# Eight gathers in a row, the gate's tiles in other PSUM banks, merge steps moved ahead of transposes

## The chip, the cores and the metric

The kernel runs on one core of one Trainium2 chip. The metric is the device time of one execution in microseconds; below it is given as the median of several executions. The core has five engines that each take their instructions in order: TensorE (PE in the profile, its weight loads PEld), VectorE (DVE), ScalarE (ACT), GpSimd (POOL) and SyncE (SP). DMAs are issued by SP, ACT or POOL, and each of these has a queue of its own.

## The reference

Attention with RMS-normalised queries and keys over 8 batches, 12 heads, 448 positions and 64 features, then a mixture of experts with a capacity: each of the 3584 tokens goes to its best expert of eight, and each expert keeps the 80 tokens with the largest gate weight. Tokens that are not kept give zero rows.

```python
def _attn_ref(q, k, v, g_q, g_k):
    q_n, k_n = rmsnorm(q, g_q), rmsnorm(k, g_k)
    scores = scale * np.matmul(q_n, k_n.transpose(0, 1, 3, 2))
    attn = softmax(scores)
    return np.matmul(attn, v)                       # x: tokens x 768 after a transpose
...
    logits = x @ w_gate
    expert_idx = np.argmax(logits, axis=1)
    gate_w = softmax(logits)[np.arange(N), expert_idx]
    for e in range(E):
        tok_idx = np.where(expert_idx == e)[0]
        if len(tok_idx) > capacity:
            keep = np.argpartition(-gate_w[tok_idx], capacity)[:capacity]
            tok_idx = tok_idx[keep]
        h = np.maximum(x[tok_idx] @ w1[e], 0.0)
        out[tok_idx] = gate_w[tok_idx, None] * (h @ w2[e])
```

## The kernel before, in words

**Attention.** Twelve heads of a batch are three groups of four, so there are 24 groups (`g`), each of seven rows of scores. The work is laid out by hand in 84 slots of two rows each, some 4.9 us long, plus a few before and after. A slot first computes the scores of its two rows (`score`, L312, into the PSUM pool `sc`, two buffers), ACT takes their exponentials (L315), DVE sums them up (`presum`, L339 and L341), and PE multiplies the rows of the slot before by `v` into `po` (`av`, L327; one buffer). Group `g` starts at slot b0 = 7g // 2, so an even group starts with a slot and an odd one in the middle of one. After its last row, ACT copies `po` to `us` (L332).

Three lists hold what else a slot does: `begins` (loads, before the scores), `mid` (between `presum` and `av`) and `end` (after `av`). The order of these lists is the program order of every engine. What matters here:

- Queries and keys of a group are prepared some slots ahead: ACT squares (L243, `mid`), DVE sums and scales them to `ms` (L252, L254), POOL raises them to the power -0.5 (`rs`, L261, at the `end` of two slots for each group), POOL multiplies (`qn`, L276, `mid`), PE transposes (`tp`, L288, `end`) into the PSUM pool `tp` (two buffers), ACT copies to `qkT` (L300, L302). The first group's squares and so on are cut in halves and spread over ACT, DVE and POOL. The gains `g_q` and `g_k` are four small DMAs from ACT's queue (L81, L82) that come after the group's first loads, and `gains` (L85) multiplies them.
- `xout` (L576 to L594) brings a group's result to rows of tokens: for `u` = 0 and then 1, four transposes of `us` into `xp` (pool `tp`), one ACT copy to `xb` (L586), and after the second, three DMAs from SP to the scratch tensor `xr_dram`. It comes at the `end` of slots b0+4 and b0+5 for an even group, b0+5 and b0+6 for an odd one. The last 64 columns of `us` are covered by the fourth transposition, which overlaps the third by 64.
- After the last group of a batch come `zl` (the logits and the sums of the softmax, L350, in the pool `tp`), its copy `zsb` (`gate1`), the transposition `zt` (`gate1t`, L365, pool `tp`) and the gate's arithmetic on DVE.
- The best 80 tokens of each expert are kept in a running list; the merge of a batch has six steps (`row`, `experts`, `own`, `counts`, `place`, `turn`) at the `end` of six slots one after the other. Each takes a PSUM buffer of the pool `sc` (`mp`) and an ACT copy out of it, and on DVE `beat` (L480, L483), `tied`, `ahead` (L514), `cnt` (L518), `put` and `keep`. They were put into the lists last, so they stand behind the slot's `rstd`, `xout` and `transp`.

**The last batch and the experts.** The last batch's gate and ranking is written out after the slots, with two buffers of `sc` for four tiles (`psb`, `pse`, `psa`, `psc`). It gives `idxT` (L798), the rows of the tokens of each expert. Then `gather` (L820) takes 80 rows of `xr_dram` by an indirect DMA from POOL's queue into `xg`, set to zero before (L815). `xpose` scales them (`xn`, L830) and transposes them (`xgT`). Two products per expert (L859, L874), the scaling `yo` (L877, three buffers) and a scatter (L882, indirect DMA from POOL's queue) follow. The scatters all write `out_dram`, so each waits for the landing of the one before.

Five of the gathers stand ahead of the first expert; the others follow one by one, each before the scatter of the expert that it stands in.

**Weights.** The first three experts' are loaded during the attention and stay. Those of the other five are brought to `wb_dram` as bf16 by POOL's queue during the attention, and fetched from there by SP (`fetch_late`) when space comes free: experts 4 and 5 by count from one at the end of the slots, the sixth's first matrix at the gate of the last batch, its second after the first `xpose` (a small `memset` of the tile sets the order), and the last two experts' after the products of the first two.

Of the kernel before, what the change touches and what calls it, by code (L numbers as in the profile page):

```python
# [20 lines left out]
def kernel(  # L21
# [50 lines left out]
    nc.scalar.activation(warm[:, 0:1], warm[:, 1:2], AF.Sqrt)  # L72
    ident = cpool.tile([128, 128], F32, name="ident")
    make_identity(nc, ident[:, :])
    identb = cpool.tile([128, 128], BF16, name="identb")
    gk2 = cpool.tile([128, 2], F32, name="gk2")
    gqk = cpool.tile([128, 1], F32, name="gqk")

    def load_g():
        for half in range(2):  # L80
            nc.scalar.dma_start(out=gk2[half * D:(half + 1) * D, 0:1], in_=g_q[:, None])  # L81
            nc.scalar.dma_start(out=gk2[half * D:(half + 1) * D, 1:2], in_=g_k[:, None])  # L82

# [122 lines left out]
    with av_stack:  # L206
# [111 lines left out]
        def av(r):  # L318
            g, x = divmod(r, RD)
            vt, at = st[g]["v"], st[g]["at%d" % x]  # L320
            if x == 0:
                st[g]["po"] = pops.tile([128, 2, 512], F32, tag="po", name="po")
            po = st[g]["po"]
            for u in range(2):
                p = slice(u * 64, u * 64 + 64)
                for hh in range(2):
                    nc.tensor.matmul(po[hh * D:(hh + 1) * D, u, :S],  # L327
                                     vt[p, hh * NX + x, :], at[p, hh, :],
                                     start=(x == 0), stop=(x == RD - 1))
            if x == RD - 1:  # L330
                st[g]["us"] = upool.tile([128, 2, S], F32, tag="us", name="us")
                nc.scalar.copy(st[g]["us"][:], po[:, :, :S])  # L332

# [9 lines left out]
        def zl(b, groups):  # L343

            if groups[0] == 0:
                gst[b]["zl"] = tpps.tile([128, 512], F32, tag="tp", name="zl")
            t = gst[b]["zl"]

            def mm(c, w, x, first, last):
                nc.tensor.matmul(t[32 * c:32 * c + 32, :S], w, x, start=first, stop=last)  # L350
            for i in groups:
                s = st[NQ * b + i]
                c = (2, 3) if i < 2 else (0, 1)
                for hh in range(2):
                    mm(hh, zsel[:, i, :], s["sm"][:, hh, :], i == 0, False)
                for u in range(2):
                    mm(c[u], wgs[:, 2 * i + u, :], s["us"][:, u, :], i == 0, i > 0)
# [4 lines left out]
        def gate1t(b):  # L362
            zt = tpps.tile([128, 512], F32, tag="tp", name="zt")
            for j in range(NJ + 1):
                nc.tensor.transpose(zt[:, j * 128:(j + 1) * 128],  # L365
                                    zsb[:, j * 128:(j + 1) * 128], ident[:, :])
            gst[b]["zt"] = zt
            if b < B - 1:
                zs = tpool.tile([128, 512], F32, tag="R", name="zs")
                nc.scalar.copy(zs[:, :], zt[:, :])  # L370
                gst[b]["zt"] = zs
# [84 lines left out]
        def merge(b):  # L456
# [80 lines left out]
            def vput():  # L537
# [6 lines left out]
                m["put"] = tpool.tile([128, NT, CAP], BF16, tag="put", name="put")  # L544
# [29 lines left out]
        def xout(g, u):  # L574
# [4 lines left out]
            for j in range(NJ + 1):  # L579
                c = j * 128 if j < NJ else S - 128  # L580
                nc.tensor.transpose(xp[:, j * 128:(j + 1) * 128], us[:, u, c:c + 128],  # L581
                                    ident[:, :])
            if u == 0:
                st[g]["xb"] = prep.tile([128, NJ + 1, 256], F32, tag="xb", name="xb", bufs=1)
            xb = st[g]["xb"]
            nc.scalar.copy(xb[:, :, u * 128:(u + 1) * 128],  # L586
                           xp[:, :].rearrange("p (j d) -> p j d", d=128))
# [4 lines left out]
            for t in range(2):  # L592
                nc.sync.dma_start(out=rows[:, t:SM // 64:2], in_=xb[64 * t:64 * t + 64, :NJ])
            nc.sync.dma_start(out=rows[:, NX - 1], in_=xb[64:, NJ])  # L594
# [52 lines left out]
        for b in range(B):  # L647
# [17 lines left out]
            for t, fs in enumerate(merge(b)):  # L665
                for f in fs:
                    at_slot(end, b0 + 8 + t, f)
# [3 lines left out]
        at_slot(begins, -10, load_g)  # L671
# [54 lines left out]
    pse = scps.tile([128, 2, 1024], BF16, tag="sc", name="pse")  # L726
# [7 lines left out]
    fetch_late(NW0 + 2, (0, ))  # L734
# [50 lines left out]
    put = tpool.tile([128, NT, CAP], BF16, tag="put", name="put")  # L785
    nc.vector.tensor_tensor(put[:], iota[:, :].unsqueeze(1).to_broadcast([128, NT, CAP]),
                            rank[:].unsqueeze(2).to_broadcast([128, NT, CAP]), op=ALU.is_equal)
    psc = scps.tile([128, 2, 512], F32, tag="sc", name="psc")
# [16 lines left out]
    NX0 = 5  # L805

    def rows(e):
        if e in (3, 4):
            return mpool.tile([CAP, XW], F32, tag="xg", name="xg")[:, :]
        return upool.tile([128, 2, S], F32, tag="us", name="xg")[:CAP].rearrange(  # L810
            "p u s -> p (u s)")[:, :XW]

    for e in range(NX0):
        xgs[e] = rows(e)
        nc.gpsimd.memset(xgs[e], 0.0)  # L815

    def gather(e):
        if e >= NX0:
            xgs[e] = rows(e)
# [24 lines left out]

    for e in range(NX0):
        gather(e)
    xpose(0)

    nc.vector.memset(w_tiles[NW0 + 2][1][:, 0, 0:2], 0.0)
    fetch_late(NW0 + 2, (1, ))  # L850
    for e in range(E):
# [15 lines left out]
        if e + NX0 < E:  # L867
            gather(e + NX0)
        DN = DM // 2
        yo = mpool.tile([CAP, DM], F32, tag="yo", name="yo", bufs=3)  # L870
# [51 lines left out]
```

## Time and profile before

| what | us |
|---|---|
| median of 3 runs | 500.81 (500.19 to 501.06) |
| the profiled execution | 498.67 |
| its span in the profile | 496.9 |
| ACT: first square of the first group (L243) starts | 6.38 |
| first scores (L312) start | 14.70 |
| `idxT` (L798) ends | 438.16 |
| first product of an expert (L859) starts | 445.89 |
| last scatter is issued (L882) | 491.77 |

The profile is of one execution. Its times are in microseconds from the start of the span; a line of the timeline has the start, the duration, the engine, the line of the program, the operation, output <- input, the shape and, in brackets, how long the engine stood idle before and what released it. A line of the groups has the total busy time, the mean of one in ns, and the idle time before them. The granted TensorE clock was 0.978 of full speed over the span.

The mean busy share of PE, 91%, is not even. In the attention, 15 to 395 us, it is busy 360.1 of 380.0 us; in the stretch of the experts, 440 to 497, 40.7 of 57.0. POOL is busy with 243.0 us in the former and 15.9 in the latter.

### The profile page before, as it was taken

How to read it: one execution, taken by the hardware profiler on the slowest of the kernel's cores; microseconds unless marked ns; L12 is line 12 of the kernel's file. 1: busy time of each engine (PE TensorE's matmuls, PEld its weight loads, DVE VectorE, ACT ScalarE, POOL GpSimd, SP SyncE). 2: the span in 40 equal slices, each digit the busy share in tenths (PEclk: the TensorE clock that was granted, in tenths of full speed). 3: DMA queues.
4: the chain of work that ended last, by engine and by line, in shares of the span. 5: the costliest groups of instructions: out<-in, count | busy, mean ns of one | idle time of the engine just before them, and what ended most of it. 6: DMA issues, size and time to landing. Idle time of an engine off the chain costs nothing. (4 is left out here: it accounts for less than half of the span.)

```text
span 496.9 us, 11200 instructions
## 1 busy us (share of the span) xinstructions
PE 451.0 (91%) x4527; PEld 222.3 (45%) x4527; DVE 358.0 (72%) x567; ACT 315.7 (64%) x491; POOL 267.7 (54%) x199
## 2 busy tenths in 40 slices
PE   6889999999899999699899999998998999869890
PEld 5334444353434444344344444443443444558770
DVE  4688756997899758776699669966976767445530
ACT  4777867877677768565787678767776666302210
POOL 2497883676555938618538835774578210242221
PEclk9799999999999999899999999999999999989996
DMA  6369979596958994994597959788939947779922
GB/s 217 117 136 300 254 184 251 97 291 183 243 121 222 230 256 74 267 162 159 172 167 247 254 166 241 188 218 200 238 98 220 211 90 264 281 214 354 372 98 60
DMA packets 68435, 100.84 MB, mean 203 GB/s; under 512 B 8480, under 2 KB 60192, under 8 KB 67104
## 3 DMA queue, kind: packets, MB, share of 16 engines
q1 hardware_dynamic: 52160, 70.54, 45.0%
q0 software_dynamic: 15616, 29.13, 32.9%
q8 instruction: 35, 0.57, 0.4%
q10 hardware_dynamic: 608, 0.46, 0.3%
q14 instruction: 16, 0.13, 0.1%
HBM read 101.12 MB, written 39.90 MB: 284 GB/s over the span
## 5 line engine op out<-in xcount | busy, mean ns | idle before, releaser
L261 POOL TENSOR_TENSOR rs<-ms,nhalf 128x14 f32<-128x14 f32 x46 | 136.5, 2970 | 130.2 <-DVE ms L254 124.0
L341 DVE TENSOR_TENSOR sm<-sm,at 128x896 f32<-128x896 f32 x120 | 155.6, 1297 | 24.1 <-ACT at L315 17.8
L315 ACT ACTIVATE at<-ps 128x896 f32<-128x896 f32 x168 | 147.8, 921 | 23.6 <-PE ps L312 19.2
L312 PE MATMUL ps<-qkT 64*64 64x448 f32 x1344 | 152.9, 561 | 9.6 <-ACT row L474 4.6
L327 PE MATMUL po<-at,vt 64*64 64x448 f32 x1344 | 145.4, 542 | 3.2 <-ACT us L332 3.2
L276 POOL TENSOR_TENSOR qn<-qk,rs 128x896 f32<-128x896 f32 (+1 forms) x45 | 84.5, 1894 | 8.3 <-DVE rs L267 8.2
L327 PEld LDWEIGHTS po<-at,vt 64*64 64x64 f32 x1344 | 50.2, 134 | 76.9 <-issue 67.0
L252 DVE TENSOR_REDUCE ms<-sq 128x14 f32<-128x896 f32 (+1 forms) x50 | 52.2, 1045 | 44.6 <-ACT sq L243 41.6
L312 PEld LDWEIGHTS ps<-qkT 64*64 64x64 f32 x1344 | 42.1, 134 | 73.7 <-issue 36.6
L288 PE MATMUL tp<-ident,qn 128*128 128x128 f32 x336 | 52.7, 280 | 5.1 <-DVE qn L276 3.5
L288 PEld LDWEIGHTS tp<-ident,qn 128*128 128x128 f32 x336 | 37.6, 142 | 32.0 <-issue 15.4
L586 ACT COPY xb<-xp 128x512 f32<-128x512 f32 x48 | 28.2, 588 | 36.6 <-PE xp L581 27.2
L243 ACT ACTIVATE sq<-qk 128x896 f32<-128x896 f32 (+1 forms) x50 | 45.9, 922 | 3.6 <-DMA qk<-in_k_dram 3.6
L581 PEld LDWEIGHTS xp<-ident,us 128*128 128x128 f32 x192 | 20.1, 140 | 34.7 <-issue 27.0
L300 ACT ACTIVATE qkT<-tp,gqk 128x512 f32<-128x512 f32 (+1 forms) x48 | 30.8, 643 | 4.7 <-PE tp L288 4.2
L302 ACT COPY qkT<-tp 128x384 f32<-128x384 f32 (+1 forms) x47 | 25.3, 538 | 12.0 <-PE tp L288 11.9
L581 PE MATMUL xp<-ident,us 128*128 128x128 f32 x192 | 31.5, 287 | 1.1 <-ACT xb L586 1.1
L863 ACT ACTIVATE h_sb<-ph 128x320 bf16<-128x320 f32 x16 | 7.0, 437 | 31.1 <-PE ph L859 31.1
L480 DVE TENSOR_SCALAR beat<-row,rg 128x128 bf16<-128x128 f32 (+3 forms) x28 | 23.2, 830 | 4.2 <-ACT row L474 3.8
L882 POOL DMA_INDIRECT out_dram<-yo,idxT x8 | 7.7, 963 | 34.2 <-DVE yo L877 14.9
L339 DVE TENSOR_TENSOR sm<-at 128x896 f32<-128x896 f32 x24 | 26.0, 1084 | 0.1
L332 ACT COPY us<-po 128x896 f32<-128x896 f32 x24 | 21.6, 902 | 5.8 <-PE po L327 5.8
(159 smaller groups left out, 407.9 us busy)
## 6 DMA issues: line engine op xcount, KB each, us to landing
wb_scratch<-in_moe_w_dram POOLq DMA_DIRECT2D x10, 1536.0 KB, 13.2
w_sb<-wb_scratch SPq DMA_DIRECT2D x10, 1536.0 KB, 11.1
vt<-in_v_dram SPq DMA_DIRECT2D x24, 448.0 KB, 6.1
out_dram<-zeros SPq DMA_DIRECT2D x28, 384.0 KB, 8.5
qk<-in_q_dram SPq DMA_DIRECT2D x23, 448.0 KB, 7.2
qk<-in_k_dram SPq DMA_DIRECT2D x23, 448.0 KB, 7.9
w_sb<-in_moe_w_dram POOLq DMA_DIRECT2D x6, 1536.0 KB, 15.3
xr_scratch<-xb SPq DMA_DIRECT2D x48, 192.0 KB, 5.5
```

The source lines that it names most:

```text
L243: nc.scalar.activation(st[g]["sq%d" % a][:, lo:hi], st[g]["qk"][a][:, lo:hi], AF.Square)
L252: nc.vector.reduce_sum(out=ms[:, lo:hi], in_=st[g]["sq%d" % a][:, lo:hi], axis=AX.X)
L261: nc.gpsimd.tensor_tensor(rs[:, lo:hi], ms[:, lo:hi], nhalf[:, lo:hi], op=ALU.pow)
L276: eng.tensor_mul(qn[:].rearrange("p (x hh) d -> p hh x d", hh=2)[:, h0:h1], qk[:, lo:hi].rearrange("p (hh x) d -> p hh x d", x=NX), rs[:, ...
L288: nc.tensor.transpose(tp[:, x * 128:(x + 1) * 128], qn[:, 2 * (x0 + x):2 * (x0 + x) + 2].rearrange("p h d -> p (h d)"), ident[:, :])
L300: nc.scalar.activation(o, i, AF.Copy, scale=gqk[:, :])
L312: nc.tensor.matmul(ps[u * 64:u * 64 + 64, hh, :S], T1[d, u, x * 64:(x + 1) * 64], T0[d, u, :], start=True, stop=True)
L315: nc.scalar.activation(at[:], ps[:, :, :S], AF.Exp)
L327: nc.tensor.matmul(po[hh * D:(hh + 1) * D, u, :S], vt[p, hh * NX + x, :], at[p, hh, :], start=(x == 0), stop=(x == RD - 1))
L341: nc.vector.tensor_add(s["sm"][:], s["sm"][:], s["at%d" % x][:])
L581: nc.tensor.transpose(xp[:, j * 128:(j + 1) * 128], us[:, u, c:c + 128], ident[:, :])
L586: nc.scalar.copy(xb[:, :, u * 128:(u + 1) * 128], xp[:, :].rearrange("p (j d) -> p j d", d=128))
```

## The change

- The four loads of the gains go from ACT's queue to POOL's, at the head of the program.
- A new tile `ul` holds the last 64 columns of both halves of `us`, copied by POOL right after `us`. One transposition of it replaces the two overlapping ones, so `xout` has four for `u` = 0 and three for `u` = 1; the copy to `xb` for `u` = 1 is 384 columns wide, not 512. The last DMA to the scratch is cut into two, since the last columns of the two halves now lie on different partitions.
- `zl` and `zt` take buffers of `sc`, not of `tp`. In the last batch `pse` and `psc` take that of `po`. `put` shares the buffer of `ahead`.
- The merge steps are put at the front of their slots' `end` lists, in the same order among themselves.
- All eight gathers stand in a row ahead of the first expert, each with a buffer of its own; the tiles for the first four are cleared by POOL, those for the last four by DVE. Both matrices of the sixth expert are fetched after the first `xpose`. `yo` has two buffers (the pool's default), not three.

```diff
@@ -70,17 +70,14 @@
     warm = cpool.tile([1, 2], F32, name="warm")
     nc.vector.memset(warm[:, :], 0.0)
     nc.scalar.activation(warm[:, 0:1], warm[:, 1:2], AF.Sqrt)
+    gk2 = cpool.tile([128, 2], F32, name="gk2")
+    gqk = cpool.tile([128, 1], F32, name="gqk")
+    for half in range(2):
+        nc.gpsimd.dma_start(out=gk2[half * D:(half + 1) * D, 0:1], in_=g_q[:, None])
+        nc.gpsimd.dma_start(out=gk2[half * D:(half + 1) * D, 1:2], in_=g_k[:, None])
     ident = cpool.tile([128, 128], F32, name="ident")
     make_identity(nc, ident[:, :])
     identb = cpool.tile([128, 128], BF16, name="identb")
-    gk2 = cpool.tile([128, 2], F32, name="gk2")
-    gqk = cpool.tile([128, 1], F32, name="gqk")
-
-    def load_g():
-        for half in range(2):
-            nc.scalar.dma_start(out=gk2[half * D:(half + 1) * D, 0:1], in_=g_q[:, None])
-            nc.scalar.dma_start(out=gk2[half * D:(half + 1) * D, 1:2], in_=g_k[:, None])
-
     def gains():
         nc.vector.tensor_mul(gqk[:, :], gk2[:, 0:1], gk2[:, 1:2])
         nc.vector.tensor_scalar_mul(gqk[:, :], gqk[:, :], 1.0 / math.sqrt(D))
@@ -330,6 +327,8 @@
             if x == RD - 1:
                 st[g]["us"] = upool.tile([128, 2, S], F32, tag="us", name="us")
                 nc.scalar.copy(st[g]["us"][:], po[:, :, :S])
+                st[g]["ul"] = prep.tile([128, 2, 64], F32, tag="ul", name="ul", bufs=1)
+                nc.gpsimd.tensor_copy(st[g]["ul"][:], st[g]["us"][:, :, SM:])
 
         def presum(r):
             g, x = divmod(r, RD)
@@ -343,7 +342,7 @@
         def zl(b, groups):
 
             if groups[0] == 0:
-                gst[b]["zl"] = tpps.tile([128, 512], F32, tag="tp", name="zl")
+                gst[b]["zl"] = scps.tile([128, 2, 512], F32, tag="sc", name="zl")[:, 0]
             t = gst[b]["zl"]
 
             def mm(c, w, x, first, last):
@@ -360,7 +359,7 @@
             nc.scalar.copy(zsb[:, :S], gst[b]["zl"][:, :S])
 
         def gate1t(b):
-            zt = tpps.tile([128, 512], F32, tag="tp", name="zt")
+            zt = scps.tile([128, 2, 512], F32, tag="sc", name="zt")[:, 0]
             for j in range(NJ + 1):
                 nc.tensor.transpose(zt[:, j * 128:(j + 1) * 128],
                                     zsb[:, j * 128:(j + 1) * 128], ident[:, :])
@@ -541,7 +540,7 @@
                 nc.vector.reduce_sum(out=rank[:], in_=rnk[:], axis=AX.X)
                 nc.vector.scalar_tensor_tensor(rank[:], rank[:], float(CAP), m["cnt"][:],
                                                op0=ALU.add, op1=ALU.subtract)
-                m["put"] = tpool.tile([128, NT, CAP], BF16, tag="put", name="put")
+                m["put"] = tpool.tile([128, NT, CAP], BF16, tag="ahead", name="put")
                 nc.vector.tensor_tensor(
                     m["put"][:], iota[:, :].unsqueeze(1).to_broadcast([128, NT, CAP]),
                     rank[:].unsqueeze(2).to_broadcast([128, NT, CAP]), op=ALU.is_equal)
@@ -576,22 +575,26 @@
             b, i = divmod(g, NQ)
             xp = tpps.tile([128, 512], F32, tag="tp", name="xp")
             us = st[g]["us"]
-            for j in range(NJ + 1):
-                c = j * 128 if j < NJ else S - 128
-                nc.tensor.transpose(xp[:, j * 128:(j + 1) * 128], us[:, u, c:c + 128],
-                                    ident[:, :])
+            for j in range(NJ):
+                nc.tensor.transpose(xp[:, j * 128:(j + 1) * 128],
+                                    us[:, u, j * 128:(j + 1) * 128], ident[:, :])
             if u == 0:
+                nc.tensor.transpose(xp[:, SM:512],
+                                    st[g]["ul"][:].rearrange("p u q -> p (u q)"), ident[:, :])
                 st[g]["xb"] = prep.tile([128, NJ + 1, 256], F32, tag="xb", name="xb", bufs=1)
             xb = st[g]["xb"]
-            nc.scalar.copy(xb[:, :, u * 128:(u + 1) * 128],
-                           xp[:, :].rearrange("p (j d) -> p j d", d=128))
+            n = NJ + 1 - u
+            nc.scalar.copy(xb[:, :n, u * 128:(u + 1) * 128],
+                           xp[:, :n * 128].rearrange("p (j d) -> p j d", d=128))
             if u == 0:
                 return
             rows = xr_dram[b * S:(b + 1) * S, i * 256:(i + 1) * 256].rearrange(
                 "(p x) d -> p x d", x=NX)
             for t in range(2):
-                nc.sync.dma_start(out=rows[:, t:SM // 64:2], in_=xb[64 * t:64 * t + 64, :NJ])
-            nc.sync.dma_start(out=rows[:, NX - 1], in_=xb[64:, NJ])
+                p = slice(64 * t, 64 * t + 64)
+                nc.sync.dma_start(out=rows[:, t:SM // 64:2], in_=xb[p, :NJ])
+                nc.sync.dma_start(out=rows[:, NX - 1, t * 128:(t + 1) * 128],
+                                  in_=xb[p, NJ, :128])
 
         def weights_early():
             qk_stack.close()
@@ -663,12 +666,11 @@
             at_slot(mid, b0 + 8, gate2i, b)
             at_slot(mid, b0 + 8, gate2p, b)
             for t, fs in enumerate(merge(b)):
-                for f in fs:
-                    at_slot(end, b0 + 8 + t, f)
+                for f in reversed(fs):
+                    end.setdefault(b0 + 8 + t, []).insert(0, (f, ()))
         at_slot(begins, 0, load_wgs)
         at_slot(end, NS - 3, weights_early)
         at_slot(end, NS, weights_late)
-        at_slot(begins, -10, load_g)
         at_slot(mid, 0, constants)
         at_slot(mid, -8, lambda: nc.scalar.activation(warm[:, 0:1], warm[:, 1:2], AF.Exp))
         for i in range(N // 128):
@@ -723,7 +725,7 @@
     gate2(b)
     gate2x(b)
     psb = scps.tile([128, 2, 512], F32, tag="sc", name="psb")
-    pse = scps.tile([128, 2, 1024], BF16, tag="sc", name="pse")
+    pse = pops.tile([128, 2, 1024], BF16, tag="po", name="pse")
     gate2i(b)
     for j in range(NT):
         nc.tensor.transpose(pse[:3 * E, 0, j * 128:(j + 1) * 128],
@@ -731,7 +733,6 @@
     eqT = tpool.tile([3 * E, 512], BF16, tag="cand", name="eqT")
     nc.scalar.copy(eqT[:, :], pse[:3 * E, 0, :512])
     gate2b(b)
-    fetch_late(NW0 + 2, (0, ))
     psa = scps.tile([128, 2, 512], F32, tag="sc", name="psa")
     gw = m["gw"]
     row = tpool.tile([128, 512], F32, tag="R", name="row")
@@ -782,10 +783,10 @@
                          m["eq"][:].rearrange("p j e -> p (j e)"))
     rank = gpool.tile([128, NT], F32, tag="rank", name="rank")
     nc.vector.reduce_sum(out=rank[:], in_=place[:], axis=AX.X)
-    put = tpool.tile([128, NT, CAP], BF16, tag="put", name="put")
+    put = tpool.tile([128, NT, CAP], BF16, tag="ahead", name="put")
     nc.vector.tensor_tensor(put[:], iota[:, :].unsqueeze(1).to_broadcast([128, NT, CAP]),
                             rank[:].unsqueeze(2).to_broadcast([128, NT, CAP]), op=ALU.is_equal)
-    psc = scps.tile([128, 2, 512], F32, tag="sc", name="psc")
+    psc = pops.tile([128, 2, 512], F32, tag="po", name="psc")
     o = psc[:CAP, 0, :2 * E]
     nc.tensor.matmul(o, identb[:CAP, :CAP], left[:].rearrange("p c e -> p (c e)"),
                      start=True, stop=False)
@@ -802,21 +803,18 @@
     mps = ctx.enter_context(tc.tile_pool(name="moe_ps", bufs=2, space=PSUM))
 
     xgs, xts, gws = {}, {}, {}
-    NX0 = 5
-
-    def rows(e):
-        if e in (3, 4):
-            return mpool.tile([CAP, XW], F32, tag="xg", name="xg")[:, :]
-        return upool.tile([128, 2, S], F32, tag="us", name="xg")[:CAP].rearrange(
-            "p u s -> p (u s)")[:, :XW]
-
-    for e in range(NX0):
-        xgs[e] = rows(e)
-        nc.gpsimd.memset(xgs[e], 0.0)
+    for e in range(E):
+        if e < 3:
+            xgs[e] = upool.tile([128, 2, S], F32, tag="us", name="xg")[:CAP].rearrange(
+                "p u s -> p (u s)")[:, :XW]
+        elif e < E - 1:
+            xgs[e] = mpool.tile([CAP, XW], F32, tag="xg", name="xg", bufs=E - 4)[:, :]
+        else:
+            xgs[e] = prep.tile([128, NJ + 1, 256], F32, tag="xb", name="xg", bufs=1)[
+                :CAP].rearrange("p j d -> p (j d)")[:, :XW]
+        (nc.gpsimd if e < 4 else nc.vector).memset(xgs[e], 0.0)
 
     def gather(e):
-        if e >= NX0:
-            xgs[e] = rows(e)
         nc.gpsimd.indirect_dma_start(
             out=xgs[e], out_offset=None, in_=xr_dram[:, :],
             in_offset=bass.IndirectOffsetOnAxis(ap=idxT[:, e:e + 1], axis=0),
@@ -842,12 +840,12 @@
         nc.vector.tensor_copy(xgT[:], pxt[:])
         xts[e] = xgT
 
-    for e in range(NX0):
+    for e in range(E):
         gather(e)
     xpose(0)
 
-    nc.vector.memset(w_tiles[NW0 + 2][1][:, 0, 0:2], 0.0)
-    fetch_late(NW0 + 2, (1, ))
+    nc.vector.memset(w_tiles[NW0 + 2][0][:, 0, 0:2], 0.0)
+    fetch_late(NW0 + 2)
     for e in range(E):
         w1_sb, w2_sb = w_tiles[e]
         h_sb = mpool.tile([128, FC, CAP], BF16, tag="hsb", name="h_sb")
@@ -864,10 +862,8 @@
                                  ph[:], AF.Relu)
         if e + 1 < E:
             xpose(e + 1)
-        if e + NX0 < E:
-            gather(e + NX0)
         DN = DM // 2
-        yo = mpool.tile([CAP, DM], F32, tag="yo", name="yo", bufs=3)
+        yo = mpool.tile([CAP, DM], F32, tag="yo", name="yo")
         for dn in range(2):
             py = mps.tile([CAP, DN], F32, tag="py", name="py")
             for fc in range(FC):
```

## The prediction

> **What bounds the kernel now.** I read the page first (busy shares, groups by line), then PE's waits, then two stretches of the timeline, then POOL and the DMA issues from 395 us on.
>
> ```profile
> span 496.9 us, 11200 instructions
> ...
> PE 451.0 (91%) x4527; PEld 222.3 (45%) x4527; DVE 358.0 (72%) x567; ACT 315.7 (64%) x491; POOL 267.7 (54%) x199
> ...
> L261 POOL TENSOR_TENSOR rs<-ms,nhalf 128x14 f32<-128x14 f32 x46 | 136.5, 2970 | 130.2 <-DVE ms L254 124.0
> ```
>
> By the table of windows PE is busy 360.1 of the 380.0 us from 15 to 395, the attention. It takes its work in program order, so a microsecond that it waits in the attention is taken as a microsecond of the span. The third line matters as much: POOL's `rs` (the power -0.5) takes 2.97 us each, and whatever is queued behind one waits that long.
>
> ```profile
> PE ps L312 <- ACT row L474: 4.6, 6, 0.9
> ...
> PE zl L350 <- ACT xb L586: 2.9, 7, 1.4
> ```
>
> These waits (total, times, longest) are what two of the edits go for. The end is another matter: the chain of waits has only the last two scatters, and before them POOL's queue goes by weights:
>
> ```profile
> 440.46 1.08 POOL L820 DMA_INDIRECT xg<-xr_scratch,idxT  x1 [10.40 <-DMA w_sb<-wb_scratch]
> ...
> 471.10 0.96 POOL L882 DMA_INDIRECT out_dram<-yo,idxT  x1 [7.34 <-DVE yo L877]
> 476.34 0.93 POOL L882 DMA_INDIRECT out_dram<-yo,idxT  x1 [4.28 <-DVE yo L877]
> 480.10 0.91 POOL L882 DMA_INDIRECT out_dram<-yo,idxT  x1 [2.83 <-issue]
> ...
> 491.77 0.91 POOL L882 DMA_INDIRECT out_dram<-yo,idxT  x1 [2.83 <-issue]
> ```
>
> Each scatter waits until the one before has landed. By the DMA issues, scatters issued at 451.5 and 461.6 took 9.2 and 8.7 us to land, that at 480.1 3.0. In between lie the weight fetches on SP's queue: issued 445.88 to 455.18, the last landed 19.7 us after its issue, at 474.9. From then scatters follow every 3.7 to 4.2 us to the end.
>
> **Gains, part by part.**
> (1) Start. ACT issues four small DMAs (1.74, 2.29, 4.92, 5.86, the last for 0.47), and its first square runs at 6.38, though the q halves had landed at 4.7 and 4.9. On POOL's queue they leave ACT free: its table is loaded at 2.53, the square starts at about 4.8. The k halves (5.9, 6.0) come in time for the third square. Gain 1.6, bounds 0 and 1.9: nothing if the gains land late, for `gqk` (10.56) already waits 0.36 for them; POOL needs some 1.0 us per issue (L171, L175), four in all, so they are out by about 5.
> (2) 24 transposes fewer, at 0.11 each (four in 0.44 at 399.53): 2.6. ACT's shorter second copy isn't PE's and costs or gains nothing.
> (3) `zl` leaves the `tp` buffers, so it no longer waits for the `xb` copy: 2.9 by PE's row, 4.6 by that of its weight loads; I take 3.8 (bounds 0, if the score buffers make it wait as long, and 4.6). `zt` waited 1.0 for the same copy, but comes right behind the `zsb` copy and its ACT result is needed as before: 0.
> (4) Merge steps first: ACT's `row` copy no longer stands behind `xb` and `qkT`, and `ps` waits less. In the odd batches the copy can be 0.65 earlier (`xp` at 135.12, `gw` ready at 134.74), in the even ones 0.24 (84.83 against 86.09, where PE is held for `gw` itself): 3 x 0.65 + 3 x 0.24 = 2.7, bounds 0 and the row's 4.6. The 4.2 for `move` are held by DVE, not by order: 0.
> Gains together 10.7.
>
> **Losses in the attention.** The 24 copies of `us`' last 64 columns go to POOL, and PE's fourth transposition of `xp` now waits for one. Alone such a copy is cheap: the nearest rows are L131's cast, 128x80 in 0.25, and `qn`, 1.89 for seven times the elements, 0.27; I take 0.3 and 0.1 to signal. The question is what is ahead of it in POOL's order. For an even group the `us` copy is in slot b0+4, and the `rs` of the slot before is ahead:
>
> ```profile
> 62.48 0.91 ACT L332 COPY us<-po 128x896 f32<-128x896 f32 x1 [0.25 <-PE po L327]
> ...
> 62.77 3.36 POOL L261 TENSOR_TENSOR rs<-ms,nhalf 128x14 f32<-128x14 f32 x1 [0.63 <-DVE ms L254]
> ...
> 64.60 0.66 PE L581 MATMUL xp<-ident,us 128*128 128x128 f32 x4
> ```
>
> `rs` ends at 66.13, the copy at 66.53; PE wants it at 64.60 + 3 x 0.11 = 64.93. PE stands 1.6 with the next scores behind it, which ACT, then `po`, wait for. So in groups 2, 8, 14 and 20: 6.4. Group 0 (`rs` 34.53 to 37.92, `xp` 36.58): 38.32 - 36.91 = 1.4. Groups 4, 10 and 16 fall in the slot of a merge step:
>
> ```profile
> 193.79 3.93 DVE L480 TENSOR_SCALAR beat<-row,rg 128x384 bf16<-128x384 f32 x1
> 194.12 3.38 POOL L276 TENSOR_TENSOR qn<-qk,rs 128x896 f32<-128x896 f32 x2
> ...
> 201.69 0.66 PE L581 MATMUL xp<-ident,us 128*128 128x128 f32 x4
> ...
> 202.79 2.79 POOL L261 TENSOR_TENSOR rs<-ms,nhalf 128x14 f32<-128x14 f32 x1 [5.29 <-DVE ms L254]
> ```
>
> A `beat` that elsewhere takes 0.3 to 0.4 was held 3.93 beside POOL's `qn`, DVE ran late, and `rs` ended at 205.58: + 0.4 - 202.02 = 4.0 for group 10, and by the same rows 4.2 and 3.3 for 4 and 16, 11.5 together, with `ahead` and `cnt` (0.48 + 0.49) ahead of `ms` a little more. If DVE's order falls so that no `beat` is held, 1.9 each, 5.7. I take 9.0, nearer to the rows. In groups 6, 12, 18 and 22 and all odd ones (their copy is used a slot later) no `rs` stands between: 0. Losses 1.4 + 6.4 + 9.0 = 16.8 (bounds 0, if the copy is out ahead of `rs`, and 1.4 + 6.4 + 11.5 + 3 x 0.97 = 22.2); the attention nets + 6.1.
>
> The Trainium skill, "SBUF — State Buffer", section "Who interferes with whom", says that VectorE's second port pair is GpSimd's too, and that whichever has it holds it for the whole instruction. The held `beat` of 3.93 agrees. By that rule the 24 copies could also each wait for a running `sm` addition (1.09), some 9 us more over the eight exposed ones; the sum goes by the rows.
>
> **The tail.** The sixth expert's first weights, issued at 433.23 and landed at 442.4, go behind the first gather. Beside them the last `rg` rows took 8.2 and 7.8 to land (at 439.2), where they took 3.6 and 3.1 at 397.6; without them the first gather, at 440.46, comes 0 to 1.4 earlier: I take 1.1 of gain. But SP now has six fetches where it had five: five took 445.88 to 474.9, 5.8 each; six from about 444.8 end at 479.6 (476.0 at 5.2 each, where less crowded by gathers). Eight gathers in a row delay no scatter (447.31 + 2 x 1.3, the first `yo` is there at 451.5). Three scatters land by about 480 beside the weights, as before at 8.7 to 9.2 each; the fourth, 476.34 before, goes at about 481, and four more follow at 3.7 to 4.2. With two `yo` buffers the product of each expert waits for the scatter two back, which gives the last one about 495.9 where it was 491.77. The fourth scatter some 5 later, less what the three gathers taken from between the scatters give: + 4.5 at the end. Bounds 0 (the stream done at 476, the fourth scatter where it was) and + 6. The `memset`s of the gather tiles hide behind the top-80's last steps (done by 432 on POOL, four of 0.75 on DVE ahead of `xn`, which waits for the gather anyway). The gate's other PSUM banks: 0, their former readers are long done.
>
> The Trainium skill, "DMA: Bandwidth & Descriptors", section "Queues, rings and completion order", says that an engine takes turns among queues packet by packet. That would make a scatter beside the weights some 2 x 3.0 = 6.0 by estimate, and the fourth would go near 474. The trace has 8.7 to 9.2; it decides.
>
> **Sum.** 496.9 - 10.7 + 16.8 + 4.5 = 507.5. The profiled execution took 498.67, 1.8 over its span, so 509.3; it was 2.1 below the median 500.81 of the three runs. Median forecast: 511.4, said as 511.
>
> **Rivals.**
> B, faster: POOL's copy isn't late. This decides if `rs` ends before `xp` is due, that is if `ms` comes some 1.6 earlier in an ordinary slot. For: the gains relieve ACT and so `sq`. Against: `rs` is in POOL's order ahead and starts within 0.3 of the `us` copy's start. Then 500.8 - 10.7 + 4.5 = 494.6.
> C, slower by less: the weights end at 476, since the gathers are through before most of them, and the tail costs nothing: 500.8 + 6.1 = 506.9. Against: the five fetches of before took 5.8 each, gathers or not.
> D, slower still: the attention and the tail at their upper bounds, the beats held and `ahead` and `cnt` in front of every exposed `ms`: 500.8 - 10.7 + 22.2 + 6 = 518.3. Against: it needs all three groups alike.
> E, it doesn't do what it says: the first gather stays at 440.4, since the wait is really the last `rg` rows' own path: tail + 5.6 (the 1.1 gone), 512.5; inside the forecast's range.
>
> **How the numbers follow.** Forecast (with E, 0.08 of it) 0.45, its own range 507.5 to 515; C 0.15; D 0.12; B 0.28, with partial forms of it (half of the stalls hidden gives 500.8 + 6.1 - 8.4 + 4.5 = 503.0, three quarters 498.8). The range for 8 in 10, 496 to 517, leaves out about half of B and half of D. A measurement tells 0.2%, 1.0 us, from no change. B gives faster in 0.25 and the same in 0.03, C and the forecast's low end same in 0.02: faster 0.25, same 0.05, slower 0.70.
>
> **What would show it.** Right: in the profile after, PE's waits name POOL `ul` with some 12 to 17 us in 8 or so times; the weight loads end past 476; fewer waits of `zl` and `ps` on `xb` and `row`. Wrong: `ul` waits under 4 us; the last scatter before 490; ACT's first square still at 6.

## The result, and the profile after

The changed kernel took 520.48 us (518.45 to 522.19, four runs) against 500.94 of the kernel before beside it: a ratio of 1.038 (1.032 to 1.044). It is slower by 19.5 us where 10.2 were forecast, and above the range, which ended at 517. The profiled execution took 522.19, its span is 520.3, so 23.4 of span have to be found: 18.7 before `idxT` ends and 4.7 after it.

The page of the changed kernel, its busy shares and one group:

```profile
span 520.3 us, 11219 instructions
...
PE 456.0 (88%) x4503; PEld 224.6 (43%) x4503; DVE 359.2 (69%) x571; ACT 315.5 (61%) x491; POOL 287.3 (55%) x226
...
L331 POOL COPY ul<-us 128x128 f32<-128x128 f32 x24 | 9.0, 375 | 94.5 <-ACT us L329 94.5
```

POOL's copies are as cheap as forecast, 0.375 us on average; POOL is not full. Yet PE does fewer instructions and has a busy time 5 us longer, at a lower share. PE's waits by what ended them (total, times, longest), the first lines:

```profile
PE xp L582 <- POOL ul L331: 20.4, 7, 4.7
PE pxt L837 <- DVE xn L828: 9.0, 3, 7.2
PE tp L285 <- POOL qn L273: 7.1, 6, 2.1
```

The first line alone has the size of the loss; in the whole list no wait of `ps` on `row` or `move` is left (4.6 and 4.2 before), and of `zl` only 0.2, on `us`. So the waits that the gains were to remove went. Others came with the new order of the merge steps: `tp` on POOL's `qn` (1.6 before), and `mp` on `eqb`, `rg`, `ahead` and `keep`, 5.8 together where it was 0.7. Here is the largest of the seven waits, in group 4, by the timelines of DVE, POOL and PE (start, duration, instruction):

```profile
103.32 0.49 DVE L517 TENSOR_REDUCE cnt<-ahead 128x4 f32<-128x320 bf16 x1
103.72 1.08 DVE L249 TENSOR_REDUCE ms<-sq 128x14 f32<-128x896 f32 x1
```

```profile
105.09 3.38 POOL L258 TENSOR_TENSOR rs<-ms,nhalf 128x14 f32<-128x14 f32 x1 [4.36 <-DVE ms L251]
108.44 0.28 POOL L331 COPY ul<-us 128x128 f32<-128x128 f32 x1
```

```profile
103.52 0.52 PE L579 MATMUL xp<-ident,us 128*128 128x128 f32 x3
108.77 0.47 PE L582 MATMUL xp<-ident,ul 128*128 128x128 f32 x1 [4.73 <-POOL ul L331]
```

`us` was ready at 101; POOL stood idle for 4.36 us, with the copy's data there and the copy next but one in its order, because the power ahead of it waited for `ms`, and `ms` stood on DVE behind `ahead` and `cnt`, which the change put there (how much of the wait is theirs, e1 shows). Then PE, back at work at 108.77, is slow. The windows around it (length, busy time and instructions of PE, PEld, DVE, ACT and POOL, then the granted clock of PE, DMA share, GB/s):

```profile
100.00:104.00 4.00, 3.45 (x51) 1.64 (x43) 3.86 (x5) 3.68 (x6) 0.73 (x1) 1.00 0.98 143
104.00:108.00 4.00, 0.04 (x1) 0.00 (x0) 3.79 (x9) 0.04 (x1) 2.91 (x1) 0.68 1.13 229
108.00:110.00 2.00, 1.23 (x8) 0.90 (x12) 1.97 (x3) 0.66 (x2) 1.56 (x3) 0.50 1.14 245
110.00:112.00 2.00, 2.00 (x12) 0.61 (x14) 1.16 (x2) 0.85 (x2) 2.00 (x1) 0.50 1.08 327
112.00:114.00 2.00, 2.00 (x24) 0.67 (x16) 1.39 (x1) 1.49 (x2) 2.00 (x2) 0.92 0.97 362
```

The clock falls to 0.50 during the stall and stays there for some 3.5 us after it (the 0.92 of the last window is 0.3 us more at 0.50): 12 matmuls in the window 110 to 112, 24 in the next. In the windows around the wait of 1.90 at 178 it is 1.00 throughout. The Trainium skill, "TensorE: Matmul & The Clock Gate", section "HAM oscillation — how this bites in real kernels", gives as a rule that PE should have no idle gaps above about 3.4 us; the waits of 4.7 and 1.9 here lie on its two sides and agree. But the border is not sharp in these traces: in this profile a wait of 2.12 at 31.6 (`tp` on `qn`) is followed by 0.50 as well, and in that of e5 one of 1.80 at 366.3 by 0.50 from 369 to 372. And the kernel before had shown the price already, behind its longest wait in the attention, 4.03 us of `ps` on `move` up to 208.41:

```profile
210.00:212.00 2.00, 2.00 (x16) 0.72 (x12) 1.97 (x2) 0.92 (x1) 2.00 (x3) 0.53 0.13 46
```

The end, from the end of `idxT` (456.87) to that of the span, is 63.4 us, where it was 58.7. POOL's timeline there:

```profile
457.75 1.09 POOL L818 DMA_INDIRECT xg<-xr_scratch,idxT  x1 [10.03 <-DVE idxT L799]
...
468.90 1.22 POOL L878 DMA_INDIRECT out_dram<-yo,idxT  x1 [1.23 <-DVE yo L873]
485.18 0.93 POOL L878 DMA_INDIRECT out_dram<-yo,idxT  x1 [15.05 <-DVE yo L873]
492.86 0.92 POOL L878 DMA_INDIRECT out_dram<-yo,idxT  x1 [6.76 <-DVE yo L873]
499.63 0.91 POOL L878 DMA_INDIRECT out_dram<-yo,idxT  x1 [5.85 <-DVE yo L873]
```

The first gather now follows `idxT` at once (0.9 after its end, 2.3 before) and the first scatter is issued 12.0 after it, not 13.4. But that scatter, beside six weight fetches and the last gathers, takes 15.5 us to land (9.2 before). DVE's timeline shows who waits for it:

```profile
484.51 1.14 DVE L873 TENSOR_SCALAR yo<-py,gws 80x384 f32<-80x384 f32 x2 [9.59 <-DMA out_dram<-yo,idxT]
```

With two `yo` buffers the third expert's scaling waits for the first scatter, and PE stands 7.2 us at `pxt` behind it; its clock is 0.50 from 485 to 490.

### The profile page after: what moved, and what is told of

Same layout as the page of the kernel before. It is cut to its first block, busy times and chain, and to the rows that moved or that the text cites. A ratio compares the mean times of both kernels' runs of the same rounds, so it can differ in the third digit from the quotient of the medians.

```text
span 520.3 us, 11219 instructions
## 1 busy us (share of the span) xinstructions
PE 456.0 (88%) x4503; PEld 224.6 (43%) x4503; DVE 359.2 (69%) x571; ACT 315.5 (61%) x491; POOL 287.3 (55%) x226
## 5 line engine op out<-in xcount | busy, mean ns | idle before, releaser
L258 POOL TENSOR_TENSOR rs<-ms,nhalf 128x14 f32<-128x14 f32 x46 | 146.5, 3189 | 70.5 <-DVE ms L251 69.1
L340 DVE TENSOR_TENSOR sm<-sm,at 128x896 f32<-128x896 f32 x120 | 161.5, 1346 | 32.6 <-ACT at L312 26.9
L312 ACT ACTIVATE at<-ps 128x896 f32<-128x896 f32 x168 | 146.1, 920 | 25.6 <-PE ps L309 22.0
L309 PEld LDWEIGHTS ps<-qkT 64*64 64x64 f32 x1344 | 44.6, 137 | 65.3 <-issue 41.8
L285 PE MATMUL tp<-ident,qn 128*128 128x128 f32 x336 | 55.0, 288 | 12.0 <-POOL qn L273 7.1
L331 POOL COPY ul<-us 128x128 f32<-128x128 f32 x24 | 9.0, 375 | 94.5 <-ACT us L329 94.5
L285 PEld LDWEIGHTS tp<-ident,qn 128*128 128x128 f32 x336 | 39.1, 145 | 31.4 <-POOL qn L273 15.4
L587 ACT COPY xb<-xp 128x512 f32<-128x512 f32 (+1 forms) x48 | 25.7, 536 | 34.7 <-PE xp L582 16.7
L873 DVE TENSOR_SCALAR yo<-py,gws 80x384 f32<-80x384 f32 x16 | 9.6, 613 | 29.4 <-DMA out_dram<-yo,idxT 14.3
L870 PE MATMUL py<-w_sb,h_sb 128*80 128x384 bf16 x128 | 26.0, 364 | 0.0
```

Of the source, the lines that this page charges most:

```text
L258: nc.gpsimd.tensor_tensor(rs[:, lo:hi], ms[:, lo:hi], nhalf[:, lo:hi], op=ALU.pow)
L285: nc.tensor.transpose(tp[:, x * 128:(x + 1) * 128], qn[:, 2 * (x0 + x):2 * (x0 + x) + 2].rearrange("p h d -> p (h d)"), ident[:, :])
L309: nc.tensor.matmul(ps[u * 64:u * 64 + 64, hh, :S], T1[d, u, x * 64:(x + 1) * 64], T0[d, u, :], start=True, stop=True)
L312: nc.scalar.activation(at[:], ps[:, :, :S], AF.Exp)
L340: nc.vector.tensor_add(s["sm"][:], s["sm"][:], s["at%d" % x][:])
L870: nc.tensor.matmul(py[:, :], h_sb[:, fc, :], w2_sb[:, fc, dn * DN:(dn + 1) * DN], start=(fc == 0), stop=(fc == FC - 1))
```

## The experiments

Each was run beside the kernel before, whose median in these batches was 500.2 to 502.1; so ratios are compared, not times alone. "Kernel before with" means one part alone.

**The copy on POOL alone (e1).**

```diff
+                st[g]["ul"] = prep.tile([128, 2, 64], F32, tag="ul", name="ul", bufs=1)
+                nc.gpsimd.tensor_copy(st[g]["ul"][:], st[g]["us"][:, :, SM:])
...
+                nc.tensor.transpose(xp[:, SM:512],
+                                    st[g]["ul"][:].rearrange("p u q -> p (u q)"), ident[:, :])
```

> The kernel before with only POOL's copy of the last columns (seven transposes for eight, four DMAs for three) and the two smaller buffer moves that make room for it. Theory A, the copy stands behind the power on POOL and that alone is the cost: PE's waits on ul come to 14 to 20 us, the three groups in a counts slot with 4.0 to 4.7 each, less 2.6 for the transposes: 12 to 18 us slower, ratio 1.024 to 1.036. Rival B, it is the merge steps ahead of ms that make the power late: the three groups wait 1.9 each, ul comes to 8 to 11, ratio 1.011 to 1.017.

Measured: 518.05, ratio 1.030 (1.023 to 1.038). Its PE waits:

```profile
PE xp L585 <- POOL ul L334: 18.8, 8, 4.1
PE ps L312 <- ACT row L476: 4.3, 6, 0.9
```

Theory A holds: the copy alone costs 3.0 of the 3.8% without any merge step moved. The waits in groups 4, 10 and 16 are 4.10, 3.87 and 3.17 here, 4.73, 4.75 and 4.70 in the changed kernel, so the order on DVE adds 0.6 to 1.5 us in each. No wait on `move` is left in e1's list, though its merge steps stand where they were: in group 10 the wait for `ul` has taken the place of the 4.0 on `move`.

**The merge steps first, alone (e2).**

```diff
-                for f in fs:
-                    at_slot(end, b0 + 8 + t, f)
+                for f in reversed(fs):
+                    end.setdefault(b0 + 8 + t, []).insert(0, (f, ()))
```

> The kernel before with only the merge steps put first. Theory A: the waits of the scores on ACT's row copy (4.6) and on move (4.2, in two places) go, and new ones come (eqb, ahead, keep, and tp on POOL's qn, together 5 to 9): between 4 us faster and 2 slower, ratio 0.992 to 1.004. Rival B, DVE's merge work ahead of ms is the larger price: 5 us slower or more, ratio 1.010 and up.

Measured: 499.91, ratio 0.996 (0.993 to 1.000). That is hardly clear of nothing. The waits on `row` and `move` are gone, 8.8 together, and another has grown from 1.6, with smaller ones behind it:

```profile
PE tp L288 <- POOL qn L276: 9.7, 9, 1.9
```

`ms`, now behind the merge on DVE, makes `rs` and `qn` late for the transposes. A gain of 2.0, near the forecast's 2.7, from another sum than forecast.

**The end alone (e3), its late weights alone (e7), and its gathers and buffers with the early weights (e11).** e3 has all edits of the end. e7 and e11 divide it:

```diff
-    fetch_late(NW0 + 2, (0, ))
...
-    nc.vector.memset(w_tiles[NW0 + 2][1][:, 0, 0:2], 0.0)
-    fetch_late(NW0 + 2, (1, ))
+    nc.vector.memset(w_tiles[NW0 + 2][0][:, 0, 0:2], 0.0)
+    fetch_late(NW0 + 2)
```

> The kernel before with only the end changed: eight gathers in a row, both matrices of the sixth expert after the first, two yo buffers. Theory A: first scatter 1.3 us earlier after the indices, but 13 to 16 us to land where it took 9.2, the third product waits for it, the last scatter is issued 57 to 60 us after the indices (53.6 before): 4 to 6 us slower, ratio 1.008 to 1.012. Rival B, the end is only late because the attention was: ratio 0.997 to 1.002.

> The kernel before with only the first matrix of the sixth expert fetched after the first gather, together with the second. Theory A, six fetches in a row in place of five are what lengthens the end: weights landed at about 480, scatters beside them 9 us and more, 3 to 5 us slower, ratio 1.006 to 1.010. Rival B, the eight gathers in a row and the two yo buffers do it: ratio 0.997 to 1.002.

> The kernel before with the eight gathers in a row and two yo buffers, but the first matrix of the sixth expert fetched where it was before. Theory A, late weights and two yo buffers each cost: with e3 2.8 slower and e7 1.1, this one 1 to 3 slower, ratio 1.002 to 1.006, with products waiting for the scatter two back. Rival B, gathers in a row help as much as the buffers cost: ratio 0.997 to 1.001.

Measured: e3 504.08, ratio 1.0058 (1.0021 to 1.0095); e7 503.15, 1.0023 (0.9995 to 1.0051); e11 502.17, 1.0043 (1.0009 to 1.0077). The late weights alone are not clear of nothing; eight gathers with two buffers cost some 2 us, and in e11's profile the third product shows it:

```profile
PE pxt L836 <- DVE xn L827: 9.1, 2, 7.3
```

So in e7 theory A's 3 to 5 us was missed, and in e3 the middle, 2.9, lies below its 4 to 6. Nor did e3's first scatter come earlier: it was issued 19.9 us after the indices and landed within 8, since DVE stood idle ahead of the first `xgT` (see the last section). In e11, with only five fetches beside it, the first scatter took 15.5 us to land, as in the changed kernel, so it is not the sixth fetch that makes it so long. The intervals of the three overlap: what each half is worth is not settled, only that the buffers and the gathers are the surer part.

**The gains on POOL alone (e4, and again as e12).**

```diff
-            nc.scalar.dma_start(out=gk2[half * D:(half + 1) * D, 0:1], in_=g_q[:, None])
+        nc.gpsimd.dma_start(out=gk2[half * D:(half + 1) * D, 0:1], in_=g_q[:, None])
```

> The kernel before with only the four small loads of the gains on POOL's queue. Theory A: the loads land at about 11.4 us, the multiplication of the gains waits 3.3 for them and PE 4.9, the first scores run at 16.1 where they ran at 14.7, and the start is 1.4 to 2.2 us longer: ratio 1.002 to 1.005. Rival B, the first square at 4.1 instead of 6.4 is kept: 1 to 1.9 us faster, ratio 0.996 to 0.998.

> The kernel of e4 once more, since it was 4.3 us faster than the kernel before while its profile shows the first scores no earlier (14.87 against 14.70). Theory A, nothing is gained at the start and the four runs of e4 fell well: 499 to 502, ratio 0.996 to 1.002. Rival B, it is really faster: 496 to 498, ratio 0.988 to 0.994.

Measured: 496.98, ratio 0.989 (0.982 to 0.996), and again 497.42, 0.994 (0.991 to 0.997). Faster both times, against theory A. But nothing shows a gain at the start: in e4 the first square is at 4.20, and then `gqk` waits for its loads, as DVE's line shows, and the first scores run at 14.87 (14.70 before).

```profile
10.57 0.16 DVE L82 TENSOR_TENSOR gqk<-gk 128x1 f32<-128x1 f32 x1 [2.47 <-DMA gk<-in_g_k_dram]
```

The start varies by as much without any edit: in the seven profiles that have these loads on ACT's queue (before, e1, e2, e3, e7, e9, e11), `gqk` starts at 10.56 to 11.95 and the first scores at 14.70 to 16.25; in the nine that have them on POOL's, at 10.06 to 11.49 and 14.19 to 16.07. So what the move does to the start is not shown. Of the 3 to 4 us the profiles of before and e4 show 1.1 at one place: before, an `xb` copy (381.12) waited 3.31 for its DMA, and in e4 (379.39) 2.18. The rest stays open; the profiled execution of e12, 498.92, is no shorter than that of the kernel before.

**The copy on ACT (e5), and the same copy asked for a slot later (e13).** Two ways to take the copy out from behind the power. In e5, from the changed kernel:

```diff
-                nc.gpsimd.tensor_copy(st[g]["ul"][:], st[g]["us"][:, :, SM:])
+                nc.scalar.copy(st[g]["ul"][:], po[:, :, SM:S])
```

and in e13 POOL keeps it:

```diff
-            at_slot(end, b0 + 4 + odd, xout, g, 0)
-            at_slot(end, b0 + 5 + odd, xout, g, 1)
+            at_slot(end, b0 + 5, xout, g, 0)
+            at_slot(end, b0 + 6, xout, g, 1)
```

> The changed kernel with the copy of the last columns taken by ACT out of po, right behind the us copy, and not by POOL. Theory A, the loss is the place in POOL's order behind the power: PE's waits on ul (20.4) go to under 2 and the time falls from 520.5 to 497 to 504, ratio 0.992 to 1.006 of the kernel before. Rival B, a copy costs as much wherever it stands, since the engine that takes it is late: 510 or more.

> The changed kernel, POOL's copy where it is, but xout of the even groups one slot later, as it is for the odd ones, so that PE asks for ul some 5 us later. Theory A, the loss is the place behind the power at the moment at which PE asks: the waits on ul go from 20.4 to under 3, the clock stays, and the time falls to 496 to 502, ratio 0.992 to 1.004. Rival B, POOL's copies disturb DVE wherever they fall, or POOL is too busy with 24 more instructions: 508 and more.

Measured: e5 495.77, ratio 0.988 (0.983 to 0.992); e13 498.46, 0.997 (0.994 to 0.999). Both are faster than the kernel before and 22 to 25 us faster than the changed one, and in their lists of PE's waits no `xp` waits for `ul` (in e5 `po` waits 3.7 for ACT's copies, where it waited 3.2 for `us`); the granted clock over the span is 0.973 and 0.983, where the changed kernel has 0.949. e13 decides the question that e5 leaves: the same 24 copies on the same engine, in the same place of its order, make PE wait no more once it asks later, and its rival B falls. It is still 0.9% slower than e5, whose time is a little below its own expectation; what the later `xout` costs was not measured.

**A stall filled with work (e6).**

```diff
+                if g in (4, 10, 16):
+                    for f in range(56):
+                        nc.tensor.matmul(xp[:, SM:512], identb[:, :], identb[:, :],
+                                         start=True, stop=True)
```

> The changed kernel with 56 small products without a reader (about 3.4 us of PE) ahead of the transposition of ul in groups 4, 10 and 16, in the 4.7 us in which PE stood. Theory A, a stall of over 4 us also costs the granted clock after it (0.55 and 0.77 in the 10 us after the one at 104): with PE kept busy these windows stay near 1.0 and the groups behind cost 1 to 2 less each, 3 to 5 us in all: 515 to 518. Rival B, only the wait counts: 519 to 522, no faster.

Measured: 514.21, ratio 1.023 (1.018 to 1.028), 6.3 us less than the changed kernel (7.5 by the ratios), more than theory A's 3 to 5. PE's timeline, and the windows at the same place:

```profile
104.11 3.29 PE L584 MATMUL xp<-identb 128*128 128x128 bf16 x56
109.00 0.33 PE L586 MATMUL xp<-ident,ul 128*128 128x128 f32 x1 [1.60 <-POOL ul L331]
```

```profile
108.00:110.00 2.00, 1.00 (x8) 0.63 (x12) 1.97 (x4) 0.59 (x2) 1.56 (x3) 1.00 1.16 241
110.00:112.00 2.00, 2.00 (x28) 0.87 (x24) 1.80 (x3) 1.84 (x3) 2.00 (x1) 1.00 1.06 289
```

`ul` comes no earlier (109.00 against 108.77), and the stall that is left and the filling together are as long as before. Only the clock differs: 1.00 for 0.50, and 28 matmuls for 12 from 110 to 112. The profiles place the gain there: from the `us` copy of group 4 to that of group 5, from 10 to 11 and from 16 to 17, e6 takes 1.7, 3.0 and 2.3 us less than the changed kernel, and up to the end of `idxT` 6.8 less in all (450.09 for 456.87). So some 6 to 7 us of the loss are not waiting but slow work after three waits.

**The gate's tiles in the score buffers, alone (e9).**

```diff
-                gst[b]["zl"] = tpps.tile([128, 512], F32, tag="tp", name="zl")
+                gst[b]["zl"] = scps.tile([128, 2, 512], F32, tag="sc", name="zl")[:, 0]
```

> The kernel before with only zl and zt in the score buffers. Theory A, as forecast: the waits of zl and zt on xb go (2.9 and 1.0), 2 to 4 us faster, ratio 0.992 to 0.996. Rival B: the waits were cover for something else that is late (the scores on row, the rows of queries), and nothing is gained: ratio 0.998 to 1.002.

Measured: 495.98, ratio 0.992 (0.988 to 0.996): 4.1 us faster, as forecast (3.8). Its profiled execution, the slowest of the five (498.66), has the first scores 1.55 later than the kernel before and the end of `idxT` 0.25 earlier, 1.8 gained between.

**Without a copy at all (e8), with the merge behind (e10) and back (e14).** `us` is written in another order, so that every block of 128 columns holds 64 of each half; seven transposes then need no copy, and two DMAs write a group.

```diff
-                nc.scalar.copy(st[g]["us"][:], po[:, :, :S])
+                nc.scalar.copy(
+                    st[g]["us"][:].rearrange("p a s -> p (a s)").rearrange(
+                        "p (x u q) -> p u x q", u=2, q=64),
+                    po[:, :, :S].rearrange("p u (x q) -> p u x q", q=64))
...
+            x0, n = (0, 4) if u == 0 else (4, NX - 4)
+            for x in range(n):
+                nc.tensor.transpose(xp[:, x * 128:(x + 1) * 128],
+                                    us[:, (x0 + x) * 128:(x0 + x + 1) * 128], ident[:, :])
```

> The kernel before with the gains on POOL, the gate's tiles in the score buffers and the merge steps first, and in place of the copy another order of us: 64 columns of one half and 64 of the other by turns, so that seven transposes serve a group without any copy and two DMAs write it, in rows of 512 bytes. No ul. Theory A: 2.6 for the transposes, 1 to 3 for the gate's tiles, 1.4 for the merge, 0 to 4 for the gains: 490 to 496, ratio 0.978 to 0.990. Rival B, twice as many packets to the scratch hold up xb, which has one buffer: 500 and more.

> The kernel of e8 with the merge steps put behind the slot's rstd, so that DVE's sums ms go ahead of beat, ahead and put again, but still ahead of the transposes of xout and of the queries. Theory A, tp's waits on POOL's qn (11.2 in e8, 1.6 before) come from ms standing behind the merge on DVE: they fall to under 5, 4 to 7 us faster than e8, 487 to 491. Rival B, they come from the slots being shorter: 492 to 495.

> The kernel of e8 with the merge steps back where they were before. Theory A, putting them first is worth about the 2 us that it was alone (the 4.0 of move and the 4.6 of row against 10 of tp on POOL's qn): 494 to 498, ratio 0.986 to 0.994. Rival B, with the shorter xout the qn waits weigh more and the old order is better: 488 to 492.

Measured: e8 493.84, ratio 0.985 (0.981 to 0.989), the fastest kernel here; e10 498.00, 0.995 (0.992 to 0.999); e14 499.29, 0.997 (0.994 to 1.000). e10's edit did not do what its expectation says: the power's entry often stands behind `xout` and the transposes in a slot's list, since it belongs to a later group, so the merge landed behind all of them. Its waits show it, and are nearly those of e14 (6.9 and 3.9):

```profile
PE ps L309 <- ACT move L536: 7.3, 2, 5.2
PE ps L309 <- ACT row L476: 4.6, 6, 0.9
```

Both are slower than either of their theories allowed. So e10 and e14 together say that the merge steps in front are worth some 5 us in this kernel (e8 against both), more than the 2 that they were alone; whether they can stand in front without making `qn` late (11.2 of waits in e8) was not tried.

## Why the prediction was wrong, point by point

The side was right (slower, 0.70), the part that decides was named, and the sum was too small by 9 us.

- **The step that failed: "I take 9.0", and with it "Losses 1.4 + 6.4 + 9.0 = 16.8".** The groups were right but for group 0, where PE did not wait. The waits are 1.27, 1.90, 1.94 and 1.10 in groups 2, 8, 14 and 20 (6.2, forecast 6.4) and 4.73, 4.75 and 4.70 in 4, 10 and 16: 14.2, where the text weighed 11.5 (a `beat` held) against 5.7 (none held, 1.9 each). Waits in all: 20.4 for 16.8. Read in the old order the 11.5 was right: e1 has 11.1. In the changed kernel no `beat` is held (the longest in the attention takes 0.58), and yet the waits came out above both: `ahead` and `cnt` stand in front of `ms`, which the text had as "a little more" and put into the bound alone, and other work of DVE was held in place of `beat`. In group 10 it is this instruction, which took 0.43 before (at 198.88) and here ran beside two `qn` of POOL:

```profile
206.23 4.37 DVE L490 TENSOR_TENSOR tied<-tied,tri 128x512 bf16<-128x512 bf16 x1
```

- **A term was missing from this step.** A wait of 4.7 was priced at its length. e6 shows 6 to 7 us on top, from a clock of 0.50 after the three long waits; the profile before had shown such a clock behind its wait of 4.03. Against this, not every microsecond of waiting was lost, as "a microsecond that it waits in the attention is taken as a microsecond of the span" had it: 20.4 + 6.3 would be 26.7, but e5 and e13, without these waits, are 24.7 and 22.0 faster. So the copy on POOL cost 22 to 25 where 16.8 was summed, 5 to 8 of the miss of 9.3, and rival D, with 22.2 for it, ended at 518.3. By e5 (1.25% faster than the kernel before) the rest of the change is worth the 6.2 that were forecast (10.7 - 4.5); by e13 (0.32%) only 1.6.
- **The parts were added up as if each stood alone.** Measured alone, the copy (e1), the merge steps (e2), the end (e3), the gains (e12) and the gate's tiles (e9) multiply to 1.017 of the kernel before, about 1.007 to 1.028 by an estimate from their intervals; the whole is 1.038 (1.032 to 1.044). One place is known: from the `us` copy of group 10 to that of 11, e2 is 4.4 shorter than the kernel before, since the wait on `move` is gone; in the changed kernel the wait for `ul` stands there (as in e1), and it is 2.0 longer. The rest is open.
- **"Gain 1.6, bounds 0 and 1.9" at the start.** No gain is seen: the first square ran at 4.08, earlier than forecast, but `gqk` (11.48) waited 3.35 for the loads, and the first scores ran at 16.07, 1.4 later than before. That too lies within what the start varies by itself (14.70 to 16.25, under e4), so its price is not shown. Why e4 and e12 are faster is open.
- **"24 transposes fewer: 2.6"** was not measured alone; e8, which has this with three other parts, is 1.5% faster than the kernel before.
- **`zl`: 3.8.** Right, alone: 4.1 (e9).
- **Merge steps: 2.7.** The size holds alone (2.0, e2, hardly clear of nothing), the working does not: "The 4.2 for `move` ... 0" was false, since this wait goes with the order, and the transposes' wait on `qn` was left out.
- **The tail: + 4.5.** The changed kernel's end is 4.7 longer. The weights were expected to end about 41 us after `idxT` (479.6 - 438.16); the last fetch lands 42 after it. The fourth scatter was expected 42.8 after it (481 - 438.16) and was issued so (499.63 - 456.87), but by another way: the first scatter's 15.5 us were not expected. Alone the end costs 2.9 (e3).
- **Rival B**, the copy hidden, is what e13 makes of the kernel, and e5 by another engine: 498.5 and 495.8 for 494.6. It needed an `xout` one slot later, or a copy that is not behind `rs`, not an earlier `ms`.

The rule weighed in the prediction from the Trainium skill, "SBUF — State Buffer", section "Who interferes with whom", bears little on the copies themselves; what was held beside POOL's work was DVE's, as `tied` above. The copies, by their line in the view of the tile (min, median, max in ns), are mostly undisturbed:

```profile
L331 POOL COPY ul<-us x24: 279/289/1042, 38.8 to 443.6; 128x128 f32<-128x128 f32 x24
```

A few are held, the longest by 0.75 us; the mean is 0.375, so all of it is about 2 us of POOL.

## What to carry to other kernels

A cheap instruction costs what stands ahead of it in its engine's order, so a copy is placed by asking which instruction it follows and when its reader asks, not by which engine has time: the same copy cost over 20 us, or no wait at all, by one slot. Where the new wait on PE may come to four microseconds (in the attention every one of 3.17 or more was followed by half the clock, and some of about 2 were), its price is the wait and the slow work behind it, and the clock's row in the windows says so. Parts that gain are best tried alone: three of the five here made the kernel 0.4 to 1.1% faster, and they were hidden under two that did not. But what parts gain alone is not what they gain together: a new wait can stand where a removed one stood.

## What had not been expected of the hardware

- After a wait of 4.73 us PE's granted clock was 0.50 for some 3.5 us more; after one of 1.90 it stayed at 1.00, after one of 2.12 it did not. Kept busy with products that nobody read, it stayed at 1.00 (e6).
- Ahead of the first copy of `xgT` DVE stood idle for 0.3 to 0.4 us in the kernel before, the changed one and e8, but for 6.67 and 6.85 us in e3 and e6, 4.00 and 4.12 in e7 and e5, and 1.66 and 2.43 in e1 and e4, whose gathers and weights are those of the kernel before. The profile names no instruction that ends this wait. It may be part of the spread of the runs; this was not tried.
- A scatter that took 3.0 us to land alone took 15.5 beside six weight fetches and the last gathers, and in e11 15.5 beside five.
